# Linear attention with a mixture of experts: turned rows moved inside the chip's memory, loads issued by ScalarE into four places, small inputs read later

## The chip, the cores and the metric

The kernel runs on one core of a Trainium2 chip. The time is that of the device, in microseconds (us), median of several runs. A core has TensorE (PE in the rows, its weight loads PEld), VectorE (DVE), ScalarE (ACT), GpSimd (POOL) and SyncE (SP), each with its own in-order instruction stream, and 16 DMA engines that all of them share. PEq, ACTq, SPq and so on are the sequencers that issue transfers and wait.

## The reference, cut to what matters

Causal linear attention with a decay per head runs over 4 batches x 8 heads x 768 positions of 64 numbers; its output, 3072 tokens of 512 numbers, goes through a mixture of 8 experts, of which each token takes the best one.

```python
# attention, block by block (the kernel uses blocks of 128)
intra = einsum('bhic,bhjc->bhij', qb, kb) * Dmask;  intra = einsum('bhij,bhjd->bhid', intra, vb)
inter = einsum('bhid,bhde->bhie', qb * lam_pow, kv_state)
out[:, :, sl] = intra + inter
kv_state = lam_block * kv_state + einsum('bhsd,bhse->bhde', kb_dec, vb)
# x = out as [3072, 512]
logits = x @ w_gate + modality_bias[modality_id]
e_idx = argmax(logits);  gate_w = softmax(logits)[e_idx]
for e in range(8):
    h = maximum(x[mask_e] @ w1[e], 0)          # 512 -> 1024
    out[mask_e] = gate_w * (h @ w2[e])         # 1024 -> 512
```

## The kernel before, in words

**Attention.** There are 24 chunks of 128 tokens, done as 12 pairs (the loop over `m`, L812 to L889). `load(m)` (L86) brings the keys, queries and values of one pair, 2 MB, into one of six places (`SLOTS`, tag `load`); SP issues all of them, the one for pair `m + 6` in iteration `m`. In iteration `m` TensorE makes the `scores` (L243) of pair `m + 1`, then `from_state` (L277) and `values` (L285) of pair `m`, then `products` (L255, the new state) of pair `m + 1`. ScalarE scales keys (`kd`, L233) and takes results out of PSUM (`xt`, L288). VectorE applies the mask (L247), adds states (L265) and turns each result in 32x32 blocks (`turn`, L294, into one of four `xn` buffers).

**From attention to tokens.** `store` (L297) writes a turned chunk to the DRAM tensor `xs`, 256 KB, issued by ScalarE; `bring` (L306) reads it back as four transfers of 64 KB per token tile `row` (128 tokens x 528 numbers, eight buffers), issued by SP. The 24 token tiles form three groups of eight. For each group the gate is worked out on TensorE (`gates`), VectorE chooses the expert and the place of each token (`choose`, `ranks`, `slots_of`), and `one_slot` (L394) on POOL scatters a tile's rows to the DRAM tensor `placed`, sorted by expert. Eight `bring`s are issued in pair 5, eight in pair 10 and eight after tile 0.

**Experts.** Then come token tiles of 256 rows of one expert: four early ones (two from list A, made when group 0 is placed, two from list B, made after group 1), two thin ones (64 and 32 rows), eight wide ones, and more under a condition. `fetch_x(n)` reads the rows `xg` from `placed`, `fetch_w1` and `fetch_w2` the weights `raw1` and `raw2` (2 MB each, in four parts; where a tile's expert is that of the tile before, the transfer is skipped by a condition). `split` (L583) cuts each weight into a high part (ScalarE) and a low part (VectorE), `first_layer` (L674) and `second` (L698) multiply in three passes (`three`, L665), and POOL scatters the result to `out`. `raw1`, `raw2`, `w1h`, `w1l`, `w2h`, `w2l` lie in the six `load` places. `late_list` (L495) makes the list of all later tiles on VectorE, in pieces between the blocks of tile 2 (`amid2`, L930); its last result is `nums`, the count that every engine reads at L1015. `clear_ends` (L616) writes blank rows behind each expert's last token, eight transfers of 528 KB, each with a register loaded from `ends_at`.

**What sets the order.** PE, DVE, ACT and SP run in the order in which the code is written. On SP every instruction stands behind the one before it, waits included. The transfers of SP and ACT share eight completion counters, handed out in turn over both engines: a transfer waits until the one eight places earlier has landed.

```python
for m in range(pairs):
    ...
    if m == 0: gpsimd_constants(); routing_constants()   # L845, needs the small inputs mod and mb
    elif m == 5: ranks(...); four bring(c)               # L854
    if m + SLOTS < pairs: load(m + SLOTS)                # L858
    if m == 5: four more bring(c)
```

Of the kernel before, what the change touches and what calls it, by code (L numbers as in the profile page):

```python
# [15 lines left out]
P = 128  # L16
# [4 lines left out]
SLOTS = 6  # L21
# [13 lines left out]
ROWS = 8  # L35
# [8 lines left out]
def linear_attention_moe(tc, qkv, lam, modality, wg, mbias, w1, w2, out):  # L44
    nc = tc.nc
    with ExitStack() as ctx:
# [51 lines left out]
        busy = const.tile([P, DM], BF16, name="busy")  # L98
# [38 lines left out]
        for m in range(4, SLOTS):  # L137
            load(m)

# [8 lines left out]
        xs = dram.tile([N, DM], F32, name="xs")  # L148
# [148 lines left out]
        def store(g):  # L297
            xn = xns.pop(g).rearrange("q t p a -> q (t p a)")
            n = P // (1 + g % HB)
            for r in range(0, P, n):  # L300
                to = g * P + (r + P - n) % P
                nc.scalar.dma_start(out=xs[to : to + n, :], in_=xn[r : r + n])

        rows = {}

        def bring(c):  # L306

            grp, tb = divmod(c, 4)
            rows[c] = work.tile([P, RW], F32, name="row", bufs=ROWS)
            for t in range(4):  # L310
                g = 4 * grp + t
                nc.sync.dma_start(out=rows[c][t * Q : (t + 1) * Q, :DM].rearrange("a (j e) -> a j e", j=4),  # L312
                                  in_=xs[g * P : (g + 1) * P, tb * P : (tb + 1) * P].rearrange("(j a) e -> a j e", j=4))
# [80 lines left out]
        def one_slot():  # L394
            c, at = slots.pop(0)
            row = rows.pop(c)
# [237 lines left out]
        def fetch_regs(n, always=False):  # L634
            _, lst, i = tiles[n]
            er = nc.sync.value_load(item(lst, 0, i), min_val=0, max_val=E - 1)
# [5 lines left out]
        def fetch_w1(er, kw, to=None):  # L642
            for i in range(4):
                nc.sync.dma_start(out=(raw1 if to is None else to)[:, i],
                                  in_=w1[bass.ds(er, 1), :, i].rearrange("o p k f -> p (o k) f"), **kw)

        def fetch_w2(er, kw, to=None):
            for i in range(4):
                nc.sync.dma_start(out=(raw2 if to is None else to)[:, i],
                                  in_=w2[bass.ds(er, 1), :, 2 * i : 2 * i + 2].rearrange("o p f n -> p (o f) n"), **kw)  # L650
# [135 lines left out]
        w1_part = lambda nm, dt: slot([P, 4, KC, TT], dt, nm)  # L786
# [3 lines left out]
        aside = {8: (0, 2), 9: (1, 2), 10: (1, 2)}  # L790
# [21 lines left out]
        for m in range(pairs):  # L812
# [10 lines left out]
            elif m == 8:  # L823
                lgt = gate_rows()
            elif m == pairs - 1:
                routed = 1, *choose(1, lgt)
            if m == 0:
                keys(2)
                keys(3)
                store(0)  # L830
                store(1)
            if ahead:
                for i, g in enumerate((a + 2, b + 2)):
# [5 lines left out]
                    if i == 0 and m > 1:  # L839
                        store(a - 1)  # L840
            elif m > 0:
                store(a - 1)
            do()
            go(aside.get(m, (0, 0))[0])
            if m == 0:  # L845
                gpsimd_constants()
                routing_constants()
            else:
                from_state((a, b))
# [4 lines left out]
            elif m == 5:  # L854
                ranks(routed[-1])
                for c in range(RC // 2):
                    bring(c)
            if m + SLOTS < pairs:  # L858
                load(m + SLOTS)
            if m == 5:  # L860
                for c in range(RC // 2, RC):
                    bring(c)
            if m == pairs - 1:
                turn_rows(0)
                fetch_x(1)
            if m > 0:
                turn(a)
                store(a)
# [11 lines left out]
            elif m == 7:  # L880
                raw1 = w1_part("raw1", F32)
                fetch_w1(*fetch_regs(0, True))
            elif m == 8:
                raw2 = w2_part("raw2", F32)
                fetch_w2(*fetch_regs(0, True))
            elif m == 10:
                fetch_x(0)
                for c in range(RC, 2 * RC):
                    bring(c)  # L889
        store(B * NC - 1)  # L890
        w2h, w2l = w2_part("w2h", F32R), w2_part("w2l", F32R)
        w1h, w1l = w1_part("w1h", F32R), w1_part("w1l", F32R)
# [10 lines left out]
        def amid0(i):  # L903
            nonlocal routed, slots, early
            if i == 0:
                ranks(routed[-1])
                slots += slots_of(*routed)
                do()
                jobs.extend([("slots", one_slot)] * RC)
            elif i == 1:  # L910
                count()
                early = early_list("B", listB, early)
            elif i == 2:
                do()

        def amid1(i):
            nonlocal routed, slots, lgt
            if i == 0:
                lgt = gate_rows()
                routed = 2, *choose(2, lgt)  # L920
# [9 lines left out]
        def amid2(i):  # L930
            if i == 0:
                late_list(*early)
            elif i < 3:
# [12 lines left out]
        need("slots")  # L946
        fetch_x(2)
        fetch_w1(*fetch_regs(2))
        for c in range(2 * RC, 3 * RC):
            bring(c)  # L950
# [12 lines left out]
        first_layer(amid2)  # L963
        fetch_w2(*fetch_regs(3))
# [3 lines left out]
        clear_ends()  # L968
# [8 lines left out]
        both1 = w1_part("both1", F32)  # L977
# [17 lines left out]
        w1h = w1_part("w1h", F32R)  # L995
# [86 lines left out]
```

## Time and profile before

| | |
|---|---|
| median of 3 runs | 469.44 us (467.18 to 471.01) |
| the profiled execution | 467.61 us, of which its span is 465.8 us |
| busy: PE, DVE, ACT, POOL | 394.3, 264.9, 195.8, 99.2 us |
| mean granted TensorE clock | 0.923 of full speed |
| DMA | 87.96 MB in 56552 packets, mean 189 GB/s |

The span is the time from the first to the last instruction of the profiled execution; the rest of its time, 1.8 us, lies around it. Busy time of PE is modelled, and an engine that is not the bottleneck may idle at no cost. A row of a timeline gives start, length, engine, line, operation, the tile written <- the tiles read, and, in brackets, how long the engine had been idle and what it had waited for.

### The profile page before, as it was taken

How to read it: one execution, taken by the hardware profiler on the slowest of the kernel's cores; microseconds unless marked ns; L12 is line 12 of the kernel's file. 1: busy time of each engine (PE TensorE's matmuls, PEld its weight loads, DVE VectorE, ACT ScalarE, POOL GpSimd, SP SyncE). 2: the span in 40 equal slices, each digit the busy share in tenths (PEclk: the TensorE clock that was granted, in tenths of full speed). 3: DMA queues.
4: the chain of work that ended last, by engine and by line, in shares of the span. 5: the costliest groups of instructions: out<-in, count | busy, mean ns of one | idle time of the engine just before them, and what ended most of it. 6: DMA issues, size and time to landing. Idle time of an engine off the chain costs nothing.

```text
span 465.8 us, 9714 instructions
## 1 busy us (share of the span) xinstructions
PE 394.3 (85%) x3501; PEld 344.9 (74%) x3501; DVE 264.9 (57%) x494; ACT 195.8 (42%) x363; POOL 99.2 (21%) x125
## 2 busy tenths in 40 slices
PE   7849998894499689278984589999999999999991
PEld 4739987773388679276972169899999989898980
DVE  6446889742368653188712057666667575757520
ACT  1507483461043623134510054646555555646410
POOL 3722334360006605500210010202020202020200
PEclk8959999998599979769997799999999999999996
DMA  7999997889658886933532930777721121210100
GB/s 268 392 406 410 406 409 222 296 240 407 172 142 283 339 247 198 298 106 141 195 123 70 287 129 1 213 250 233 236 65 46 46 48 46 45 46 1 47 24 20
DMA packets 56552, 87.96 MB, mean 189 GB/s; under 512 B 9134, under 2 KB 34222, under 8 KB 56496
## 3 DMA queue, kind: packets, MB, share of 16 engines
q1 hardware_dynamic: 48928, 68.19, 44.4%
q0 software_dynamic: 3920, 12.78, 7.1%
q10 hardware_dynamic: 3648, 6.29, 3.8%
q8 instruction: 29, 0.48, 0.4%
q14 instruction: 27, 0.22, 0.1%
HBM read 96.86 MB, written 24.13 MB: 260 GB/s over the span
## 4 chain that ended last, share of the span: by engine, by line
issue 48%; DMA 26%; DVE 6%; POOL 6%; PE 5%; SPq 4%; ACT 2%; POOLq 0%; ACTq 0%; DVEq 0%
DMA raw<-in_w_dram 9%; DMA load<-in_qkv_dram 8%; POOL out_dram L710 5%; DMA row<-xs 5%; DMA xs<-xn 3%; SPq L312 3%; PE s L686 2%; DVE w2l L585 2%; PE kv L686 2%; DMA xg<-placed 1%; DVE hl L694 1%; ACT kd L233 1%; ACT w2h L584 1%; PE o L285 1%; PE s L243 1%
## 5 line engine op out<-in xcount | busy, mean ns | idle before, releaser
L585 DVE TENSOR_TENSOR w2l<-raw,w2h 128x1024 fp32r<-128x1024 f32 x48 | 58.8, 1224 | 51.0 <-ACT w2h L584 51.0
L666 PE MATMUL o<-w2h,hh 128*128 128x512 f32 x192 | 75.1, 391 | 0.0
L668 PE MATMUL o<-w2h,hl 128*128 128x512 f32 x192 | 74.9, 390 | 0.0
L667 PE MATMUL o<-w2l,hh 128*128 128x512 f32 x192 | 74.9, 390 | 0.0
L710 POOL DMA_INDIRECT out_dram<-y,idx x24 | 30.9, 1287 | 204.9 <-ACT y L709 175.4
L666 PE MATMUL kv<-xh,w1h 128*128 128x256 f32 x176 | 51.9, 295 | 11.4 <-DVE hl L694 11.4
L584 ACT CAST w2h<-raw 128x1024 fp32r<-128x1024 f32 x48 | 49.9, 1040 | 26.9 <-DMA raw<-in_w_dram 15.2
L585 DVE TENSOR_TENSOR w1l<-raw,w1h 128x1024 fp32r<-128x1024 f32 x44 | 51.1, 1220 | 5.2 <-ACT w1h L584 4.9
L667 PE MATMUL kv<-xl,w1h 128*128 128x256 f32 x176 | 51.5, 293 | 0.0
L666 PE MATMUL s<-xh,w1h 128*128 128x256 f32 x176 | 50.6, 288 | 1.0 <-ACT w1h L584 1.0
L668 PE MATMUL kv<-xh,w1l 128*128 128x256 f32 x176 | 51.2, 291 | 0.0
L668 PE MATMUL s<-xh,w1l 128*128 128x256 f32 x176 | 50.4, 286 | 0.8 <-DVE w1l L585 0.8
L667 PE MATMUL s<-xl,w1h 128*128 128x256 f32 x176 | 50.4, 286 | 0.0
L666 PEld LDWEIGHTS kv<-xh,w1h 128*128 128x128 f32 x176 | 35.0, 199 | 15.4 <-DVE hl L694 11.6
L584 ACT CAST w1h<-raw 128x1024 fp32r<-128x1024 f32 x44 | 43.0, 1046 | 3.3 <-DMA raw<-in_w_dram 3.3
L233 ACT ACTIVATE kd<-load,dk 128x64 f32<-128x64 f32 x144 | 35.9, 334 | 16.8 <-DMA row<-xs 6.5
L668 PEld LDWEIGHTS o<-w2h,hl 128*128 128x128 f32 x192 | 36.0, 188 | 7.6
L667 PEld LDWEIGHTS o<-w2l,hh 128*128 128x128 f32 x192 | 36.2, 188 | 7.2
L666 PEld LDWEIGHTS o<-w2h,hh 128*128 128x128 f32 x192 | 36.2, 188 | 7.2
L668 PEld LDWEIGHTS kv<-xh,w1l 128*128 128x128 f32 x176 | 35.3, 201 | 0.0
L666 PEld LDWEIGHTS s<-xh,w1h 128*128 128x128 f32 x176 | 33.8, 192 | 2.0 <-ACT w1h L584 1.4
L667 PEld LDWEIGHTS kv<-xl,w1h 128*128 128x128 f32 x176 | 35.1, 199 | 0.0
(217 smaller groups left out, 619.8 us busy)
## 6 DMA issues: line engine op xcount, KB each, us to landing
raw<-in_w_dram SPq DMA_DIRECT2D x104, 512.0 KB
load<-in_qkv_dram SPq DMA_DIRECT2D x9, 2048.0 KB
row<-xs SPq DMA_DIRECT2D x96, 64.0 KB
xg<-placed SPq DMA_DIRECT2D x48, 128.0 KB
placed<-blank SPq DMA_DIRECT2D x9, 528.0 KB
load<-in_qkv_dram SPq DMA_DIRECT2D x8, 512.0 KB
both<-in_w_dram SPq DMA_DIRECT2D x8, 512.0 KB
xs<-xn ACTq DMA_DIRECT2D x12, 256.0 KB
```

Of the source, the lines that this page charges most:

```text
L233: nc.scalar.activation(out=kds[g][:, p, hl, :], in_=kn[:, p, hl, :], func=AF.Copy, scale=dk[:, hl, p, P - 1 : P])
L243: nc.tensor.matmul(scs[g][:, hl, p, :], kt[r, p, :], qt[r, p, :], start=True, stop=True)
L285: nc.tensor.matmul(op[place(g, hl), p, :], vt[:, (2 * p + hl) * D : (2 * p + hl + 1) * D], pt[:, hl, p, :], start=(c == 0 and p == 0), sto ...
L312: nc.sync.dma_start(out=rows[c][t * Q : (t + 1) * Q, :DM].rearrange("a (j e) -> a j e", j=4), in_=xs[g * P : (g + 1) * P, tb * P : (tb + 1 ...
L584: nc.scalar.copy(out=hi, in_=src)
L585: nc.vector.tensor_tensor(out=lo, in0=src, in1=hi.bitcast(F32), op=ALU.subtract)
L666: nc.tensor.matmul(out, ah, bh, start=first, stop=False)
L667: nc.tensor.matmul(out, ah, bl, start=False, stop=False)
L668: return nc.tensor.matmul(out, al, bh, start=False, stop=last)
L686: mm = nc.tensor.matmul(hp[:, j, :], raw1[:, i, kc, fs], xt2[:, kc, :], start=(kc == 0), stop=(kc == KC - 1))
L694: nc.vector.scalar_tensor_tensor(out=hl[a][:, b], in0=hp, scalar=0.0, in1=hh[a][:, b].bitcast(F32), op0=ALU.max, op1=ALU.subtract)
L710: sc = nc.gpsimd.indirect_dma_start(out=out, out_offset=bass.IndirectOffsetOnAxis(ap=idx[:, t, 0:1], axis=0), in_=y, in_offset=None, bound ...
```

## The change

- `store` and `bring` go, and with them `xs`, `row` and their buffers. `spread(g)` copies a turned chunk straight from its `xn` buffer into the token tiles of its group, in the chip's memory: four transfers of 64 KB, each [32 partitions, 4, 128 numbers], issued by SP for every chunk as it is turned. A group's eight token tiles are one buffer (`grp`, three of them).
- `SLOTS` is 4 instead of 6. Pairs 0 to 3 are loaded by SP, pairs 4 to 11 by ScalarE, the one for pair `m + 4` in iteration `m`. `w1h`, `w1l` and `both1` take `grp` buffers. The first weights are fetched by ScalarE, one transfer of 2 MB each, in pairs 8 and 9 instead of by SP in pairs 7 and 8.
- `routing_constants` moves from pair 0 to pair 2; group 0 is scattered in pairs 7 to 9 instead of 8 to 10; group 1 is chosen in pair 8 and scattered in pair 11 (before: chosen in pair 11 and scattered during tiles 0 and 1). List B is made in pieces in tile 0.
- `clear_ends` stands ahead of `fetch_w2` of tile 3 instead of behind it, and `late_list` starts one block earlier in tile 2.

```diff
-SLOTS = 6
+SLOTS = 4
 def load(m):
     ...
-        nc.sync.dma_start(out=halves[m], in_=source(m))
+        (nc.sync if m < SLOTS else nc.scalar).dma_start(out=halves[m], in_=source(m))
-for m in range(4, SLOTS):
-    load(m)
-def store(g): ...
-def bring(c): ...
+def group(g):
+    n = B * NC // RN
+    if g % n == 0:
+        groups.append(work.tile([P, 2 * 4 * RW], F32, name="grp", tag="grp", bufs=RN))
+    return groups[g // n].rearrange("p (g c w) -> p g c w", g=2, c=4)[:, g % n // 4]
+def spread(g):
+    to = group(g)
+    xn = xns.pop(g).rearrange("q t p a -> q t (p a)")
+    t = g % 4
+    for j in range(4):
+        i = j ^ 2 * (g % HB)
+        nc.sync.dma_start(out=to[t * Q : (t + 1) * Q, :, i * P : (i + 1) * P], in_=xn[j * Q : (j + 1) * Q])
...
-aside = {8: (0, 2), 9: (1, 2), 10: (1, 2)}
+aside = {7: (1, 1), 8: (1, 2), 9: (1, 2), 11: (4, 4)}
...
     if m == 0:
         gpsimd_constants()
-        routing_constants()
     else:
+        if m == 2:
+            routing_constants()
...
-    elif m == 7: ... fetch_w1(*fetch_regs(0, True))
+    elif m == 8: ... fetch_w1(*fetch_regs(0, True, nc.scalar), eng=nc.scalar)
-    elif m == 8: ... fetch_w2(*fetch_regs(0, True))
+    elif m == 9: ... fetch_w2(*fetch_regs(0, True, nc.scalar), eng=nc.scalar)
...
 fetch_w1(*fetch_regs(2))
-for c in range(2 * RC, 3 * RC):
-    bring(c)
 first_layer(amid1)
 fetch_w2(*fetch_regs(2))
...
 first_layer(amid2)
+clear_ends()
 fetch_w2(*fetch_regs(3))
 turn_rows(3)
 split_rows()
 split_w1()
-clear_ends()
```

ScalarE in the middle of the attention loop, before (`xs<-xn` are the stores, `kd` the scaled keys, `xt` the results taken out of PSUM):

```order
L288 COPY xt<-o 128x512 x2
L302 DMA xs<-xn 128x512
L233 ACTIVATE kd<-load,dk 128x64 x8
L302 DMA xs<-xn 64x512 x2
L233 ACTIVATE kd<-load,dk 128x64 x8
```

and now, at the same place and up to the first weights (`raw_1378` is `raw1`):

```order
L283 COPY xt<-o 128x512 x2
L88 DMA load<-in_qkv_dram 128x4x1024
L228 ACTIVATE kd<-load,dk 128x64 x16
L334 ACTIVATE l<-l 128x64
L283 COPY xt<-o 128x512 x2
L631 TENSOR_LOAD listA
L631 ISA x2
L640 ISA
L640 DMA raw_1378<-in_w_dram 128x4096
```

Three stores a pair have left ScalarE's stream, and one load of 2 MB has come in behind the two copies.

SP from its first loads to the rows of tile 0, before:

```order
L89 DMA load<-in_qkv_dram 128x4x1024 x5
L613 DMA placed<-blank 256x1x528
L89 DMA load<-in_qkv_dram 128x4x1024 x2
L312 DMA row<-xs 32x4x128 x16
L89 DMA load<-in_qkv_dram 128x4x1024
L312 DMA row<-xs 32x4x128 x16
L636 TENSOR_LOAD listA
```

and now (`grp<-xn` are the spreads):

```order
L134 DMA mod<-in_modality_dram 128x48
L135 DMA mb<-in_mbias_dram 128x16
L308 DMA grp<-xn 32x4x128 x24
L608 DMA placed<-blank 256x1x528
L308 DMA grp<-xn 32x4x128 x60
L594 TENSOR_LOAD listA
```

The loads and the weights of tile 0 no longer stand between SP's small transfers.

SP in tile 2, before (`raw_1364` is `raw2`; the last part of `fetch_w2` of tile 3, then the clears):

```order
L649 DMA raw_1364<-in_w_dram 128x1024
L619 TENSOR_LOAD ends_at
L619 ISA x2
L613 ISA
L613 DMA placed<-blank 256x1x528
L619 TENSOR_LOAD ends_at
L619 ISA x2
L1015 TENSOR_LOAD nums
L1015 ISA x2
L613 ISA
L613 DMA placed<-blank 256x1x528
```

and now (`raw_1378` is `raw1`; the last part of `fetch_w1` of tile 3, then the clears):

```order
L643 DMA raw_1378<-in_w_dram 128x1024
L614 TENSOR_LOAD ends_at
L614 ISA x2
L608 ISA
L608 DMA placed<-blank 256x1x528
L614 TENSOR_LOAD ends_at
L614 ISA x2
L1008 TENSOR_LOAD nums
L1008 ISA x2
L608 ISA
L608 DMA placed<-blank 256x1x528
```

In both the read of `nums` stands behind the first of the eight clears; now the four parts of `fetch_w2` of tile 3 come after the eighth.

## Rows read from the trace of the kernel before

**Rows 1.** Stretches of 10 us: length, busy time by engine, granted clock, DMA share, GB/s

```profile
60.00:70.00 10.00, 9.93 (x188) 8.79 (x189) 8.18 (x15) 8.52 (x32) 3.72 (x3) 1.00 1.03 409
70.00:80.00 10.00, 8.80 (x188) 7.62 (x185) 9.45 (x31) 3.68 (x11) 5.09 (x7) 1.00 0.71 220
...
90.00:100.00 10.00, 7.38 (x99) 5.82 (x97) 3.28 (x8) 5.59 (x21) 4.85 (x6) 1.00 0.71 215
```

**Rows 2.** Timeline of SP in the attention stage and in tile 0

```profile
58.53 20.75 SPq L312 DMA_DIRECT2D row<-xs  x16
79.45 0.39 SPq L89 DMA_DIRECT2D load<-in_qkv_dram  x1
80.44 18.36 SPq L312 DMA_DIRECT2D row<-xs  x16
...
119.43 16.68 SPq L312 DMA_DIRECT2D row<-xs  x32
```

**Rows 3.** Timeline of TensorE in the attention stage

```profile
30.55 1.97 PE L277 MATMUL o<-qd,state 64*64 64x128 f32 x28 [6.75 <-DVE state L265]
...
99.67 2.06 PE L243 MATMUL s<-load 64*128 64x128 f32 x32
...
112.77 1.66 PE L319 MATMUL x<-xt,wgq 128*32 128x128 f32 x28 [3.82 <-ACT xt L288]
122.37 6.35 PE L686 MATMUL s<-xt,raw 128*128 128x256 f32 x16 [7.94 <-DVE xt L654]
```

**Rows 4.** Timeline of TensorE, tiles 2 and 3 and the first thin tile

```profile
180.35 0.28 PE L666 MATMUL s<-xh,w1h 128*128 128x256 f32 x1
...
200.51 0.58 PE L666 MATMUL kv<-xh,w1h 128*128 128x256 f32 x1 [11.36 <-DVE hl L694]
218.09 0.39 PE L666 MATMUL s<-xh,w1h 128*128 128x256 f32 x1 [0.99 <-ACT w1h L584]
...
251.29 5.38 PE L726 MATMUL s<-raw,xf 128*64 128x256 f32 x32 [8.03 <-DMA raw<-in_w_dram]
260.22 0.59 PE L726 MATMUL s<-both,xf 128*32 128x256 f32 x2 [3.54 <-DMA both<-in_w_dram]
```

**Rows 5.** DMA queues, of the page: packets, MB, share of 16 engines

```profile
q10 hardware_dynamic: 3648, 6.29, 3.8%
```

**Rows 6.** Stretches, columns as in rows 1: brings alone, then the first layer of tile 0

```profile
131.00:134.00 3.00, 3.00 (x16) 2.55 (x16) 2.27 (x6) 1.47 (x2) 1.15 (x1) 1.00 0.47 134
...
122.40:139.20 16.80, 16.80 (x75) 14.17 (x75) 9.67 (x29) 5.63 (x7) 1.15 (x1) 0.84 0.54 156
```

**Rows 7.** Chain that ended last: start, length, what; weights of tile 0

```profile
106.46 10.43 DMA raw<-in_w_dram
```

**Rows 8.** Timeline of SP, from tile 2 to the thin tiles

```profile
208.59 1.34 SPq L649 DMA_DIRECT2D raw<-in_w_dram  x4
210.75 24.34 SPq L613 DMA_DIRECT2D placed<-blank  x8
237.67 2.25 SPq L602 DMA_DIRECT2D xq<-placed  x4
```

**Rows 9.** Chain that ended last, in tile 2: late_list between the splits

```profile
200.46 0.07 DVE cntC L339
...
202.63 1.22 DVE w2l L585
...
204.46 0.09 DVE fewer L339
...
206.26 1.23 DVE w2l L585
207.48 0.60 DVE hl L694
...
214.38 0.17 DVE nums L339
```

**Rows 10.** Timeline of ScalarE at the end of tile 1

```profile
180.55 0.69 ACT L709 ACTIVATE y<-o,idx 128x512 f32<-128x512 f32 x1 [2.72 <-PE o L668]
```

More of the change, by code (lines that the diff above doesn't have):

```diff
@@ L96, in linear_attention_moe @@
             load(m)
-        busy = const.tile([P, DM], BF16, name="busy")
+        busy = work.tile([P, 2 * DM], BF16, name="busy", tag="qd", bufs=4)[:, :DM]
         nc.vector.memset(busy, 0.0)
@@ L295, in turn @@
                                 in_=xts[g].rearrange("q p (t a) -> q p t a", t=4))
[L297 to L313, printed above, removed]
+        groups = []
+        def group(g):
[10 more added lines that the diff above has]
+                nc.sync.dma_start(out=to[t * Q : (t + 1) * Q, :, i * P : (i + 1) * P], in_=xn[j * Q : (j + 1) * Q])
         def gates(grp):
@@ L395, in one_slot @@
             c, at = slots.pop(0)
-            row = rows.pop(c)
+            row = group(c // 4 * 4)[:, c % 4]
             pool(nc.gpsimd.tensor_copy(out=row[:, DM:].bitcast(I32), in_=pay[:, c, :]))
@@ L784, in keep_busy, with w1_part @@
                 nc.tensor.matmul(nothing, busy[:, :P], busy, start=(i == 0), stop=(i == n - 1))
-        w1_part = lambda nm, dt: slot([P, 4, KC, TT], dt, nm)
+        def w1_part(nm, dt, own=False):
+            if own:
+                part = work.tile([P, 2 * 4 * RW], dt, name=nm, tag="grp", bufs=RN)
+                return part[:, : 4 * KC * TT].rearrange("p (a k f) -> p a k f", a=4, k=KC)
+            return slot([P, 4, KC, TT], dt, nm)
         w2_part = lambda nm, dt: slot([P, 4, 2, DM], dt, nm)
         pairs = B * NC // HB
-        aside = {8: (0, 2), 9: (1, 2), 10: (1, 2)}
+        aside = {7: (1, 1), 8: (1, 2), 9: (1, 2), 11: (4, 4)}
         keep_busy(9)
@@ L829, in linear_attention_moe @@
                 keys(3)
-                store(0)
-                store(1)
+                spread(0)
+                spread(1)
             if ahead:
@@ L839, in linear_attention_moe @@
                     if i == 0 and m > 1:
-                        store(a - 1)
+                        spread(a - 1)
             elif m > 0:
-                store(a - 1)
+                spread(a - 1)
             do()
@@ L853, in linear_attention_moe @@
                 clear(slice(E * CAP, E * CAP + TT))
-            elif m == 5:
+            elif m == 5 or m == 9:
                 ranks(routed[-1])
-                for c in range(RC // 2):
-                    bring(c)
             if m + SLOTS < pairs:
                 load(m + SLOTS)
[L860 to L865, printed above, removed]
             if m > 0:
                 turn(a)
-                store(a)
+                spread(a)
             if ahead:
@@ L879, in linear_attention_moe @@
                 count()
-            elif m == 7:
+            elif m == 8:
                 raw1 = w1_part("raw1", F32)
-                fetch_w1(*fetch_regs(0, True))
-            elif m == 8:
+                fetch_w1(*fetch_regs(0, True, nc.scalar), eng=nc.scalar)
+            elif m == 9:
                 raw2 = w2_part("raw2", F32)
-                fetch_w2(*fetch_regs(0, True))
+                fetch_w2(*fetch_regs(0, True, nc.scalar), eng=nc.scalar)
             elif m == 10:
                 fetch_x(0)
-                for c in range(RC, 2 * RC):
-                    bring(c)
-        store(B * NC - 1)
+        turn_rows(0)
+        spread(B * NC - 1)
+        fetch_x(1)
         w2h, w2l = w2_part("w2h", F32R), w2_part("w2l", F32R)
-        w1h, w1l = w1_part("w1h", F32R), w1_part("w1l", F32R)
+        w1h, w1l = w1_part("w1h", F32R, True), w1_part("w1l", F32R, True)
         hh = [work.tile([P, 2, 2, TT], F32R, name=f"hh{i}", tag="pt", bufs=4) for i in range(2)]
```

55 lines of the change are left out of this document (27 added, 28 removed).

## The prediction

> **What bounds the kernel now.** I read the stretches first, then SP's timeline, then TensorE's waits, then the chain. Two points in time carry the sum: T0, the start of tile 0 on TensorE at 122.4 us, and T2, the start of tile 2 at 180.35 [rows 3, 4]. The wide tiles at the end keep TensorE full, and the change doesn't touch them.
>
> Up to T0 the DMA engines are the bound, with holes. From 60 to 70 us their share is 1.03 at 409 GB/s: full. From 70 to 80 and from 90 to 100 it is 0.71 [rows 1]. In these holes SP is going through brings, 16 in 20.75 us and 16 in 18.36, and the last load of 2 MB leaves only at 79.45, between them [rows 2]. Against a share of 1.00 the holes are 2 x 10 x 0.29 = 5.8 us. TensorE had stood still for 6.75 us before 30.55, for a VectorE that waited for the small inputs, and for 7.94 us before T0, for the rows of tile 0 [rows 3]. Those rows were asked for behind the weights, which landed at 106.46 + 10.43 = 116.9 [rows 7].
>
> From T2 to the first thin tile SP is the bound. Tile 2 stops for 11.36 us in its second block, since `fetch_w2` of tile 2 stands on SP behind 32 brings. Then the clears take SP 24.34 us, to 235.1, and only at 237.67 come the thin rows; the thin tile waits 8.03 us for its turn and then for `both1` [rows 4, 8].
>
> **The change part by part.**
>
> *DMA work up to T0.* The stores go: 6.29 MB in 3.8% of 465.8 us is 17.7 us of all engines, 0.74 per chunk [rows 5]. The eight brings of group 0 go: brings alone ran at 134 GB/s with a share of 0.47, so 285 GB/s at a full one, 0.92 us per chunk, 7.4 in all [rows 6]. 24 spreads come in. No row shows a transfer from on-chip memory to on-chip memory. The nearest is the bring, of the same 64 KB in the same 512-byte pieces to the same 32 partitions; below it stands the rate of the loads, 0.64 per chunk [rows 1], above it the pace at which SP got 16 brings out while loads were in flight, 18.36 / 4 = 4.6 per chunk [rows 2]. I take 0.92: 22.1 us. Net: 22.1 - 17.7 - 7.4 = -3.0.
>
> The 512-byte bring ran at 285 GB/s where the large loads ran at 409 [rows 1, 6]. The Trainium skill (DMA: Bandwidth & Descriptors, Specifications) gives 512 bytes as the size from which line rate is reached; this trace does not agree. By the page's rule the spreads would cost 24 x 0.64 = 15.4 us and the sum would be 6.7 lower.
>
> *The holes.* With the loads on ScalarE's queue none waits behind SP's small transfers. I book the 5.8 us as regained. What could take them: a load now waits for its place (four instead of six) and for the transfer eight places earlier, and behind it on ScalarE stand the scaled keys, for which TensorE's `products` wait. Between nothing and all, I take all, since the place of pair m is needed again only in pair m + 3.
>
> The Trainium skill (DMA: Bandwidth & Descriptors, Issuing engines are not separate DMA queues) says that issuing from several engines saves only the sequencer's issue time. Here a load took SP 0.39 us to issue, but stood behind 20.75 us of brings [rows 2], which the page doesn't count. By the rule the move of eight loads is worth 8 x 0.39 = 3.1 us instead of 5.8.
>
> *The rows of tile 0.* The weights leave SP for ScalarE, so the rows are not asked for behind them. The gates end at 112.77 + 1.66 = 114.4 [rows 3]; of the wait behind them the part up to 116.9 goes, 2.5 us, and the transfer itself stays. Tile 0 thus starts 3.0 + 5.8 + 2.5 = 11.3 earlier, at T0 = 111.1.
>
> *Small inputs later.* VectorE no longer waits for them in pair 0, and the 6.75 us of TensorE go. I count nothing for it: DMA is full there, and the loads are late next. Its price shows in the pace. Before, nine pairs took from 30.55 to 99.67, 7.7 us each, and T0 came 22.7 after that, 20.2 without the 2.5. Now the nine start at 23.8, and 111.1 - 20.2 - 23.8 = 66.9 leaves 7.4 per pair. If DMA were not the bound, the gates would end at 114.4 - 6.75 - 3.82 = 103.9, and T0 can't come sooner [rows 3].
>
> *Tile 0.* Its first layer ran at a mean clock of 0.84 over 16.8 us [rows 6]: after the wait TensorE worked at 1.2 instead of 2.4 GHz for a while, which cost 16.8 x 0.16 = 2.7 us. The wait shrinks from 7.9 to 5.4; I take half, 1.3. The scatters of group 1 now stand on POOL before T0; nothing on POOL is due before the result of tile 0, and the rows of tile 1 have the 14 us of tile 0's first layer. Tile 1 I leave as it is.
>
> *Tile 2 and the clears.* With no brings on SP, `raw2` is there at T2. The late list starts one block earlier, and its end, `nums`, sets SP free: it reads `nums` behind the first clear. VectorE: the result of tile 1 leaves ScalarE 0.9 after T2 [rows 10], and a cast of at most 1.2 follows: 2.1. Then four times a split and a low part, 1.23 + 0.60 each, 7.3. Then the list, 2.17 + 1.80 + 6.47 = 10.4 between the splits [rows 9]. `nums` is ready at T2 + 19.8. From `nums` (214.55) to the end of the clears (235.1) it took 20.5: T2 + 40.3. Now `fetch_w2` of tile 3, skipped, stands behind: 1.34 for its four parts [rows 8] and register reads, at most the 2.6 between the last clear and the thin rows; the thin rows go out at T2 + 44.2. Before it was 237.67 - 180.35 = 57.3. Gain 13.1.
>
> This has a price: tile 3 cannot split `raw2` before about T2 + 42.9, so TensorE stands still there for some 14 us, in place of the 11.36 in tile 2. From a stall of this kind to the end of tile 2 it took 218.09 - 200.51 = 17.6 with three blocks to go [rows 4]. With one block to go, and some 3.7 us of casts ahead of it (estimated from rows 9), tile 3 ends by T2 + 64 at the latest, and the first thin layer (5.38) by T2 + 69. `both1` used to come 260.22 - 237.67 = 22.6 after the thin rows, now T2 + 66.8. So SP's row is the later one, or TensorE by up to 2 us; I book nothing.
>
> *The rest at nothing:* `busy` in a shared buffer, w1 parts in `grp` buffers (their scatters are over 20 us before), one transfer for 2 MB of weights, and group 2's brings, which lie inside the stall already counted.
>
> **Sum.** 11.3 + 1.3 + 13.1 = 25.7. Against the profiled execution, 467.6 (span 465.8 and 1.8 around it), that makes 441.9; the median of the runs is 1.8 higher, so I forecast 443.
>
> **Rivals.**
>
> *The spreads run at the rate of the large loads.* For: nothing has to come from DRAM. Against: the brings' 285 GB/s. 443 - 6.7 = 436. This is the page's rule on 512 bytes as this kernel would show it.
>
> *The loads gain issue time only.* For: the DMA engines are shared, and four places bind the loads as the brings did. Against: the load at 79.45. 443 + 2.7 = 446. It is what the page's rule on issuing engines gives.
>
> *The clears are not held by `nums`.* They would start about T2 + 5, end by T2 + 29 and let tile 3 go: some 11 us earlier, 432. Against: the order, where the read of `nums` stands behind the first clear.
>
> *The spreads get the pace of the brings among loads*, 4.6 per chunk, 9.2 per pair [rows 2]. T0 = 23.8 + 9 x 9.2 + 20.2 = 126.8, 4.4 later than before, 15.7 than forecast: 459. For: SP still issues 96 of them, each waiting for the one eight places earlier, often a load. Against: they are spread over all pairs now.
>
> *Slower: loads and spreads of a pair run one after the other*, through the eight shared counters: the spread waits for the load, the next load on ScalarE for the spread, and the keys behind it. A load is 2.1 MB at 409 GB/s, 5.1 us; two chunks of spreads take 4.2 (32 brings in 16.68 without loads) to 9.2 [rows 1, 2]; a pair then 9.3 to 14.3, middle 11.8. T0 = 23.8 + 106.2 + 20.2 = 150.2, 39.1 later than forecast: 482. It decides from 10.8 per pair, where T0 is at 141.5 and the other gains of 14.4 and 1% are eaten.
>
> **How the numbers follow.** About 1% is what a measurement of this kernel can tell from no change. Chances: forecast 0.45, issue time only 0.13, spreads at load rate 0.12, clears free 0.05, pace of the brings 0.15, one after the other 0.10. All but the last two are faster by over 1% (below 465), and two thirds of the pace case: 0.85. The rest of that case, 0.05, is within 1%; 0.10 is slower. The range takes in the load-rate case, most of the free clears and most of the pace case: 427 to 462. Bounds of the spread's price lie inside it.
>
> **What would show it.** Right: tile 0 starts at 105 to 117; shares near 1 from 20 to 100 us; no TensorE wait near the second pair's state; no stall in the second block of tile 2; one of about 14 us in tile 3, ended by `raw2`; thin rows on SP some 44 us after T2. Wrong: spreads that take well over 1 us of all engines per chunk, ScalarE's keys waiting for landings in every pair, or tile 3 running through.

## The result, and the profile after

The changed kernel takes 473.73 us (median of 4 runs, 473.02 to 474.57), the kernel before, beside it, 468.97 (4 runs, 467.18 to 471.01): ratio 1.0101, 95% interval 1.0055 to 1.0147. It is about 1% slower; 443 was forecast, with 427 to 462 as the range.

TensorE after (timeline; columns as in [rows 3, 4]):

```profile
24.39 2.08 PE L238 MATMUL s<-load 64*128 64x128 f32 x16 [3.96 <-DMA load<-in_qkv_dram]
...
127.92 1.06 PE L314 MATMUL x<-xt,wgq 128*32 128x128 f32 x26 [0.34 <-ACT xt L283]
...
140.63 6.59 PE L688 MATMUL s<-xt,raw 128*128 128x256 f32 x16 [11.65 <-DVE xt L656]
...
197.94 0.28 PE L668 MATMUL s<-xh,w1h 128*128 128x256 f32 x1
...
245.26 0.58 PE L668 MATMUL kv<-xh,w1h 128*128 128x256 f32 x1 [13.57 <-DVE hl L696]
```

Tile 0 starts at 140.63 (T0), 18.3 later than before [rows 3]: the gates end at 129.0 instead of 114.4, and the wait behind them has grown from 7.9 to 11.65. From there on the kernel is quicker: T0 to the end of the span takes 330.7 instead of 343.4. Tile 2 starts at 197.94 (T2), with no stall in its second block [rows 4]; tile 3 stalls for 13.57.

SP after (timeline; `grp<-xn` are spreads, the eight `placed<-blank` the clears, `xq` the thin rows, [rows 2, 8]):

```profile
57.43 75.86 SPq L308 DMA_DIRECT2D grp<-xn  x60
134.66 1.93 SPq L597 DMA_DIRECT2D xg<-placed  x4
...
137.28 7.85 SPq L308 DMA_DIRECT2D grp<-xn  x12
...
177.07 6.28 SPq L651 DMA_DIRECT2D raw<-in_w_dram  x4
...
210.96 27.63 SPq L608 DMA_DIRECT2D placed<-blank  x8
240.43 1.21 SPq L651 DMA_DIRECT2D raw<-in_w_dram  x4
242.49 1.94 SPq L597 DMA_DIRECT2D xq<-placed  x4
```

The thin rows go out 242.49 - 197.94 = 44.55 after T2, against 57.3 before. The rows of tile 0 (`xg`) leave at 134.66, behind a row of 60 spreads that ends at 133.3.

The 10-us stretches after, to set beside [rows 1]:

```profile
60.00:70.00 10.00, 5.68 (x94) 4.87 (x91) 4.81 (x11) 3.14 (x11) 2.49 (x2) 0.90 0.85 232
70.00:80.00 10.00, 10.00 (x139) 8.72 (x137) 5.85 (x13) 3.84 (x15) 1.46 (x2) 0.76 0.80 253
...
90.00:100.00 10.00, 7.16 (x134) 5.92 (x133) 6.00 (x24) 1.20 (x4) 4.73 (x8) 1.00 1.00 334
```

The holes have not gone but spread: 232 GB/s at a share of 0.85 from 60 to 70 us, where it was 409 at 1.03. The whole stretch from 20 us to T0, first before, then after:

```profile
20.00:122.37 102.37, 77.31 (x1432) 67.48 (x1428) 62.55 (x156) 43.16 (x149) 31.18 (x34) 0.91 0.94 340
20.00:140.63 120.63, 93.53 (x1436) 80.75 (x1433) 63.79 (x160) 43.19 (x150) 31.64 (x36) 0.88 0.88 269
```

Share times length is the work of all DMA engines: 96.2 us before, 106.2 after. The rest, 6.1 and 14.5, they stood idle. So of the 18.3 us some 10 are more DMA work and some 8 more idle time.

Who waits, from 20 to 130 us (engine, line, releaser: total us, times, longest):

```profile
SPq L308 <- DMA load<-in_qkv_dram: 23.9, 7, 7.2
SPq L308 <- DMA grp<-xn: 23.7, 9, 4.8
...
ACT kd L228 <- DMA grp<-xn: 47.9, 8, 8.8
```

SP's spreads wait for loads, and ScalarE's scaled keys, behind a load in ScalarE's stream, wait for spreads, in every pair. So the loads come 10.9 us apart:

```profile
34.24 0.41 ACTq L88 DMA_DIRECT2D load<-in_qkv_dram  x1
...
99.60 0.38 ACTq L88 DMA_DIRECT2D load<-in_qkv_dram  x1
```

(the second load on ScalarE and the eighth, 65.4 us for six steps.) This is the picture of the slower rival. The question of the experiments: is it the waits of the transfers for one another, the price of the spreads on the DMA engines (the time for which these are busy with them), the places, or the queue they stand in?

### The profile page after: what moved, and what is told of

Its sections match the earlier page's. It is cut to its first block, busy times and chain, and to the rows that moved or that the text cites. A ratio compares the mean times of both kernels' runs of the same rounds, so it can differ in the third digit from the quotient of the medians.

```text
span 471.3 us, 9647 instructions
## 1 busy us (share of the span) xinstructions
PE 405.5 (86%) x3501; PEld 354.6 (75%) x3501; DVE 264.2 (56%) x494; ACT 194.7 (41%) x363; POOL 99.5 (21%) x125
## 4 chain that ended last, share of the span: by engine, by line
issue 47%; DMA 19%; PE 11%; DVE 8%; POOL 6%; SPq 4%; ACT 2%; POOLq 0%; ACTq 0%; DVEq 0%
DMA grp<-xn 8%; POOL out_dram L712 5%; DMA mod<-in_modality_dram 5%; DMA load<-in_qkv_dram 4%; SPq L308 2%; DMA placed<-blank 2%; PE s L688 2%; ACT kd L228 2%; PE o L668 2%; PE o L669 2%; PE o L670 2%; PE kv L688 1%; DVE pt L242 1%; DVE w2l L580 1%; DVE hl L696 1%
## 5 line engine op out<-in xcount | busy, mean ns | idle before, releaser
L580 DVE TENSOR_TENSOR w1l<-raw,w1h 128x1024 fp32r<-128x1024 f32 x44 | 51.3, 1222 | 4.5 <-ACT w1h L579 4.3
L668 PEld LDWEIGHTS kv<-xh,w1h 128*128 128x128 f32 x176 | 34.9, 198 | 17.6 <-DVE hl L696 13.8
L289 DVE STREAM_TRANSPOSE xn<-xt 128x512 f32<-128x512 f32 x24 | 17.0, 709 | 44.3 <-ACT xt L283 24.7
L250 PE MATMUL kv<-load,kd 128*64 128x64 f32 x320 | 31.1, 259 | 7.9 <-ACT kd L228 7.9
L215 POOL TENSOR_TENSOR qd<-load,pq 128x512 f32<-128x512 f32 x20 | 25.2, 1271 | 58.9 <-DMA load<-in_qkv_dram 41.9
```

The source lines that it names most:

```text
L215: pool(nc.gpsimd.tensor_tensor(out=qds[g], in0=loaded(g)[1], in1=pq, op=ALU.mult))
L250: nc.tensor.matmul(kp[r, g % HB, p, :], kd[:, p, hl, :], vt[:, (2 * p + hl) * D : (2 * p + hl + 1) * D], start=True, stop=True)
L289: nc.vector.transpose(out=xns[g].rearrange("q t p a -> q p t a"), in_=xts[g].rearrange("q p (t a) -> q p t a", t=4))
L580: nc.vector.tensor_tensor(out=lo, in0=src, in1=hi.bitcast(F32), op=ALU.subtract)
L668: nc.tensor.matmul(out, ah, bh, start=first, stop=False)
```

## The experiments

Unless said otherwise an experiment is an edit of the changed kernel and one run, and every timeline is one profile; "gates" is the end of the last gate matmul, T0 the start of tile 0: 129.0 and 140.6 there. Runs 1, 5 to 7, 9, 10, 13 and 18 don't give the experts the right rows; they serve the timing alone. Theory and rivals stand in the expectations, which were written before each group of runs.

**1. A quarter of the bytes.**

```diff
...
-out=to[t * Q : (t + 1) * Q, :, i * P : (i + 1) * P], in_=xn[j * Q : (j + 1) * Q]
+out=to[t * Q : (t + 1) * Q, :1, i * P : (i + 1) * P], in_=xn[j * Q : (j + 1) * Q, :1]
```

> Each of the 96 spreads carries a quarter of its bytes (one of the four rows of 512 bytes per partition; the rest of the row tiles is filled with zeros by VectorE, three fills); their number, order, queue and waits stay. The rows that the experts get are thus wrong in three quarters; the routing is not. Theory A (the eight shared completion counters pass loads and spreads on one after the other): the chain of waits stays as long as its landings, so tile 0 starts at 130 to 140 us, against 140.6. Theory B (the spreads' traffic itself: some 1.2 us of all DMA engines per chunk, and loads slowed beside them from 5.1 to 6.2 us): 24 x 1.2 x 0.75 = 21.6 us and most of 8 x 1.1 go, tile 0 starts at 110 to 119, and loads run at 380 GB/s or more of a full share.

Gates 114.2, T0 123.5, 457.25 us. T0 lies between the two theories: the bytes matter, but 9.3 us of wait for tile 0's rows are left.

**2. Loads with counters of their own.** `nc.scalar` becomes `nc.gpsimd` for loads 4 to 11.

> Loads 4 to 11 are issued by GpSimd, whose transfers have completion counters of their own; spreads stay on SP, all else too. No load waits for a spread any more, no spread for a load, and ScalarE's keys stand behind neither. Theory A (shared counters): the waits of SP for loads (24 us) and of ScalarE's keys for spreads (48 us) go, the pace falls from 10.9 to the 8.6 per pair that the DMA engines need (6.2 for the load, 2.4 for two chunks), so tile 0 starts near 140.6 - 9 x 2.3 = 120. Theory B (traffic): the DMA engines were at a share of 0.9 anyway; tile 0 starts at 134 to 141.

Gates 129.7, T0 138.6, 471.88 us: no gain at the gates. By itself this speaks against A. But something else waits now (SP, then VectorE, whose turn needs an `xn` buffer that a spread still reads):

```profile
SPq L310 <- DMA grp<-xn: 27.0, 22, 4.0
...
DVE xn L291 <- DMA grp<-xn: 20.6, 6, 6.1
```

Eight spreads a pair still share eight counters among themselves. And there was little idle time to win: from 20 us to the gates the share of the DMA engines is 0.95, against 0.91 in the changed kernel.

**3. Loads on SP again.** `nc.sync` for all loads.

> Loads 4 to 11 are issued by SP again, at the same place of the program, with four places as before. ScalarE's keys no longer stand behind a load that waits. Theory C (the waits of the keys behind the loads are the loss): TensorE's 7.9 us of waits for keys go, tile 0 starts near 132. Theory A: the counters still tie loads to spreads, in one queue now: 138 to 148. Theory B: the same traffic, 137 to 143.

Gates 143.4, T0 148.2, 483.02 us: later, at the end of A's range. C gets no support, but this is no clean test of it: the loads now stand behind the spreads on SP, and TensorE waits 31.4 us for loads, the keys 28.7.

**4. The price of a spread alone.** 32 transfers `away[t] <- made[j]` on SP in the third wide tile.

> 32 transfers of the spreads' form (64 KB each, from 32 partitions to 32 partitions of another quarter, in pieces of 512 bytes) are added on SP in the third wide tile, where the DMA engines are nearly idle: their price alone. Booked in the forecast: 0.92 us of all engines per four transfers, 285 GB/s at a full share. Theory A: 270 to 300 GB/s at a full share (the rest is waits). Theory B: 190 to 230 GB/s at a full share. The time of the whole kernel within 2 us of the changed kernel's.

```profile
344.00:354.00 10.00, 10.00 (x50) 8.45 (x49) 6.67 (x8) 6.22 (x8) 1.81 (x1) 1.00 0.48 115
```

115 / 0.48 = 240 GB/s, 1.09 us of all engines per 262 KB, between the two theories; the pieces turned out to be 2 KB, and 8 of the 32 transfers stay in their own partitions, so it isn't quite the spread. The whole took 482.4, not within 2 us, since the next weights stood behind the probe. Its attention part is that of the changed kernel, and its gates ended at 129.6 and its T0 was 144.1: between single profiles a few us of T0 mean nothing.

**5. Pieces of 2 KB.** `out=to[t * Q : (t + 1) * Q, i, :DM]`, one row.

> The changed kernel with each spread writing its four pieces of 512 bytes of a partition as one piece of 2 KB, into one row (so rows of the experts are wrongly put together; bytes, number, queue, order and waits of the spreads stay). Theory P (the small pieces make the spreads dear, 128 of them in each transfer): the mix of loads and spreads runs near the 400 GB/s of the loads alone, and tile 0 starts at 116 to 128 us. Theory S (traffic between two places on the chip is dear whatever its pieces): tile 0 within 4 us of 140.6. The probe alone, whose pieces turned out to be 2 KB, moved 103 GB/s at a share of about 0.42, 245 at a full one, which speaks for S.

Gates 125.1, T0 135.5, 467.41 us: T0 lies in neither range. Small pieces may cost something, not most.

**6. The source in DRAM.** `in_=w2[g % E, j * Q : (j + 1) * Q, :4, :P]`.

> The changed kernel with each spread reading 64 KB of w2 in DRAM, in the same pieces of 512 bytes to the same partitions, instead of the turned rows (which are left out of the row tiles; a spread then no longer waits for VectorE's turn). Theory S (source on the chip is what costs): spreads at the price of a bring, 0.92 us per chunk, tile 0 at 120 to 130 us. Theory P or any small transfer into 32 partitions beside loads: the mix stays at 300 to 335 GB/s at a full share, tile 0 at 136 to 144.

Gates 145.5, T0 146.4, 475.66 us. Up to T0 SP's queue took 29.0% of 126.4 = 36.7 us, (36.7 - 10.0) / 23.2 = 1.15 per chunk with the 10.0 of run 7 taken off, where the same working gives 1.28 for the changed kernel (below). So T0 is not late because both ends lie on the chip.

**7. No spreads.** The `for j` loop of `spread` goes.

> The changed kernel without the spreads: the row tiles are filled with zeros by VectorE (three tiles, two fills each), so the experts get empty rows. What remains up to tile 0 are loads, four places and TensorE's own work (75 us of it between 30 and 120 us before the change). Theory B (the spreads' traffic and what it does to the loads): loads land early, TensorE is the bound, tile 0 starts at 104 to 114 us, against 123.5 with a quarter of the bytes. Rival F (four places instead of six and the loads on ScalarE cost much by themselves): tile 0 at 118 or later.

```profile
108.63 1.06 PE L315 MATMUL x<-xt,wgq 128*32 128x128 f32 x26 [0.34 <-ACT xt L283]
110.56 3.72 PE L689 MATMUL s<-xt,raw 128*128 128x256 f32 x16 [0.87 <-DVE xt L657]
```

T0 110.56, 441.77 us. All 30 us of T0 come with the spreads; without them the four places, the loads on ScalarE and the later small inputs leave T0 within 0.6 of the forecast. F falls.

**8. The change's tile part on the kernel before.** The late list one block earlier, the second weights of tile 2 by ScalarE.

> The kernel before with its attention part (stores, brings, six places, loads on SP) and two things of the change's tile part: the late list begins one block earlier, and the second weights of tile 2 don't stand behind the brings of group 2 (one transfer of 2 MB, issued by ScalarE). The clears stay where they were. My theory of tile 2 (11.4 us of stall go; the list's end sets the clears free at about 20 us into tile 2, so that the thin rows go out 44 us into it, against 57 before): 13 us less, 452 to 458 us, ratio 0.965 to 0.98. Rival G (the brings of group 2 and their scatters hold the clears or the rows of tile 3 instead): 463 us or more, ratio 0.985 or above.

468.93 us (10 runs), ratio 1.0009 (0.9973 to 1.0045): nothing won. The stall in tile 2 went, but the brings now took SP 28.7 us, and tile 3 waited 7.2 for its weights and the first thin tile 15.3. The rival holds.

**9. Edits 1 and 2 together.**

> Both earlier edits together: spreads with a quarter of their bytes (rows three quarters zeros) and loads 4 to 11 issued by GpSimd with completion counters of their own. Without spreads tile 0 started at 110.6, with a quarter of the bytes at 123.5 although the DMA engines then had a share of only 0.78, with full bytes and loads on GpSimd at 138.6. Theory D (two limits close together: the chain load, spread, load through the counters, and the DMA time of the mix; taking one away alone leaves the other): with both gone tile 0 starts at 110 to 117. Rival (the counters don't matter, small transfers cost by their number): 120 to 126.

Gates 112.7, T0 119.7 (3.8 earlier than in run 1), 452.82 us. T0 lies between the two expectations, at the edge of the rival's. Not settled.

**10. All 128 partitions.** `nc.sync.dma_start(out=to[:, t, j * P : (j + 1) * P], in_=xn[:, j])`.

> The changed kernel with each spread of 64 KB going from 128 partitions to the same 128 partitions, one piece of 512 bytes each, instead of four pieces from 32 partitions to 32 others (rows of the experts are wrongly put together; bytes, pieces, number, queue and order stay). Theory K (all pieces of a transfer meet in a quarter of the partitions): spreads near 0.7 us per chunk, loads beside them near 370 GB/s, tile 0 at 118 to 128. Theory N (what counts is the number of small pieces, 512 of them per chunk): tile 0 at 137 to 144, spreads at 1.2 to 1.3 us per chunk.

Gates 123.0, T0 133.3, 466.12 us. With the pieces over all partitions the gates end 6.0 earlier (one profile on each side); K explains a part.

**11. Brings of group 2 earlier, in the kernel before.** Six of its eight rows ahead of `fetch_x(2)`, and the late list as in 8.

> The kernel before with two edits, all on its own queues: the late list begins one block earlier, and of the 32 brings of group 2 the first 24 are issued before the rows and first weights of tile 2, when SP has nothing else to do but wait for the scatters of group 1; the last 8 stay. In the run with loads of tile 2 by ScalarE the brings took SP 28.7 us instead of 20.2 and nothing was won. Theory (SP's queue in tile 1 is the limit; the second weights of tile 2 leave at about 177 instead of 190, the 11.4 us of stall become 0 to 3, the thin rows go out 44 to 47 us into tile 2): 453 to 460 us, ratio 0.967 to 0.985. Rival (the brings, each behind a scatter, push the rows of tile 2 back and TensorE waits there instead): 464 to 472, ratio 0.99 to 1.01.

466.44 us (10 runs), ratio 0.9978 (0.9951 to 1.0004). The thin rows left 4.4 us earlier than before, but tile 2 still stalled, for 8.2: the rows of tile 2 now left SP at 169.2, its second weights at 185.8. Nearly the rival.

**12. Tile 0's rows by GpSimd.**

```diff
...
+            if m == pairs - 1:
+                turn_rows(0)
...
-                fetch_x(0)
-        turn_rows(0)
+                fetch_x(0, nc.gpsimd)
```

> The changed kernel with the rows of tile 0 fetched by GpSimd (its queue holds no spreads, and the scatters of group 0 end on it at 106 us) instead of by SP behind 80 spreads, and turned by VectorE before the last two chunks instead of behind them. Theory (the 11.65 us that TensorE waits for tile 0 are SP's queue of spreads: gates end at 129.0, the last spread ahead of the rows leaves at 133.3, the rows land at 139.3): the wait falls to 1 to 3 us, tile 0 starts at 130 to 132, and the whole is 5 to 10 us shorter than the changed kernel, ratio to before 0.987 to 1.0; the pace of the pairs stays. Rival (the rows of tile 1, behind the last spreads and the scatters of group 1, take the wait over): tile 0 earlier, but tile 2 within 3 us of 197.9, ratio to before 1.005 to 1.015.

464.62 us (10 runs), ratio to before 0.9914 (0.9875 to 0.9953): the best complete kernel of the series.

```profile
133.82 1.06 PE L314 MATMUL x<-xt,wgq 128*32 128x128 f32 x26 [0.19 <-ACT xt L283]
134.81 3.72 PE L688 MATMUL s<-xt,raw 128*128 128x256 f32 x16
```

Tile 0 follows the gates without a wait. (They ended 5.9 later in this profile than in that of the changed kernel.) T2 is 189.6, 8.4 earlier. So the wait at T0 came from SP's row of spreads.

**13. Six places.**

> The changed kernel with six places for the loads, as before, and all spreads with their full bytes, form and order. The memory for it comes from the row tiles: all spreads write into one tile of four rows, and the scatters take an empty row, so the experts get empty rows; the parts of w1 lie in the places again, as before. The wait for tile 0's rows stays on SP behind the spreads. Theory P (the DMA time of the spreads as such: in five runs the gates end later by 0.58 us for each us of DMA time added to the run without spreads): gates end at 125 to 131, against 129.0 with four places. Theory F (four places hold no load in reserve, so that each delay of a load reaches TensorE; with six the loads run ahead as before): gates end at 112 to 119.

Gates 144.8, 505.16 us: unclear. The scatters, which share one row here, held GpSimd up and through its `qd` TensorE (12.8 us in one place), and VectorE waited 29.2 for spreads into the one shared tile. It gives no support to F, and no clean number.

**14. Clears behind the second weights of tile 3**, on top of 12.

> The run with tile 0's rows fetched by GpSimd, and the clears put back behind the second weights of tile 3. Forecast's step (tile 3's stall of 13 us behind the clears lies beside SP's own row of clears and thin rows and costs nothing, or up to 2 us): the stall goes, a wait of 8 to 14 us for the first thin tile's weights comes in its place, time within 3 us of that run's 464.6, ratio to before 0.985 to 0.996. Rival (the stall was the path): 455 to 459, ratio 0.97 to 0.98.

468.24 us (12 runs), ratio 0.9973 (0.9939 to 1.0006). The stall in tile 3 went, 9.2 of wait for the thin weights came in its place, the thin rows left 44.6 after T2 as ever: the tiles behave as forecast. It is 3.6 us slower than run 12: in its profile the gates, where the program doesn't differ, ended 5 later, after two waits of ScalarE before its last copies out of PSUM, 7.55 and 4.00 us, which the profile puts down to "remote"; in run 12 they are 4.50 and 1.13, for TensorE. Each comparison with before stands; the difference of the two I don't read. From T0 to the end of the span the two take 329.0 (14) and 330.3 (12).

**15. Spreads for group 0 only**, on top of 12; groups 1 and 2 by stores and brings.

> The run with tile 0's rows on GpSimd, with spreads for the 8 chunks of group 0 alone. Groups 1 and 2 go to DRAM by stores (SP, 0.74 us per chunk) and come back by brings into row tiles of their own: group 1 behind the attention part, group 2 behind the second weights of tile 1. Theory P (the DMA time of the spreads, 1.36 us per chunk with what they cost the loads, delays the gates by 0.58 of it; stores of before by 0.19): gates end at 109.7 + 0.58 x 10.8 + 0.19 x 11.8 = 118, tile 0 starts at 118 to 122, the whole takes 450 to 458 us, ratio 0.96 to 0.977. Rival (places and queues hold the pairs back, whatever carries the rows): gates at 126 or later, 460 us or more.

466.61 us (10 runs), ratio 0.9951 (0.9915 to 0.9988). Gates 119.2, T0 120.5, as worked out. In one kernel the two kinds of stretch stand side by side, first pairs with spreads, then pairs with stores:

```profile
30.00:70.00 40.00, 32.17 (x564) 28.70 (x561) 22.53 (x50) 15.17 (x53) 9.25 (x8) 0.93 0.82 233
90.00:110.00 20.00, 16.17 (x339) 14.51 (x337) 18.11 (x54) 9.95 (x38) 10.52 (x14) 1.00 1.02 401
```

The second stretch carries weights, since the last load left at 87.59. The loads alone leave 11.4 us apart beside spreads (34.38 to 68.60, three steps); the next three steps, beside stores, are 2.1, 10.0 and 7.0.

The whole won less than hoped: the brings came back on SP: stalls of 4.5 and 6.7 us in tiles 1 and 2, thin rows 51.3 after T2.

**16. Stores only**, the brings of group 0 among pairs 3 to 6.

> The same without any spread: all chunks by stores on SP, the brings of group 0 two rows per pair in pairs 3 to 6. Theory P: gates end at 110 + 0.19 x 25 = 114.5 as before the change, tile 0 at 115 to 119, 447 to 456 us, ratio 0.953 to 0.972. Rival (places and queues): gates at 124 or later, 458 us or more.

478.34 us (4 runs), ratio 1.0197 (1.0132 to 1.0261), gates 136.3. A clear miss: theory P, a price in DMA time, doesn't carry. Up to T0 the DMA engines do about the work of before (0.84 x 116.2 = 97.6 us, against 96.2), yet the gates end 22 us later. Eight brings stood in each of four pairs, between a load and the next, and these loads left 12.6 us apart (41.37 to 91.84, four steps). But one wait in the 22 us has another cause:

```profile
129.16 1.97 PE L272 MATMUL o<-qd,state 64*64 64x128 f32 x28 [10.18 <-POOL qd L215]
```

GpSimd made this `qd` late, behind the fetch of tile 0's rows, for which it had waited 12.32 us until scatters landed. So up to 10 us belong to the place of that fetch. Brings and spreads have in common that they are many; this run alone doesn't show that it is their number.

**17. 48 brings by GpSimd**, on top of 15.

> The run with spreads for group 0 alone, with 16 of the 32 brings of group 1 and all 32 of group 2 issued by GpSimd, with counters of its own; SP keeps 16. Theory (SP's queue in the tiles was what took the gain back): the weights of tiles 1 and 2 leave SP when their places are free, the stalls of 4.5 and 6.7 us go, tile 2 starts near 120.5 + 57 = 178, the thin rows leave 45 us later at 223, 452 to 459 us, ratio 0.963 to 0.98. Rival (the transfers themselves, 29 us of DMA time on top of the weights and rows, or GpSimd's own order, hold the tiles up): stalls in tile 1 or 2 stay, 463 us or more.

467.06 us (8 runs), ratio 0.9949 (0.9914 to 0.9984). The thin rows left at 230.05, 5.9 earlier than in 15 but 7 later than hoped, tile 1 stalled 6.4 for its weights' low part. Then some 5 us more were lost at the very end, as told in the last section.

**18. One transfer for a chunk instead of four**, on top of 10.

```diff
-for j in range(4):
-    nc.sync.dma_start(out=to[:, t, j * P : (j + 1) * P], in_=xn[:, j])
+nc.sync.dma_start(out=to[:, :, t * P : (t + 1) * P], in_=xn)
```

> The run whose spreads went between the same 128 partitions (e10_wide), with the four transfers of a chunk made one: 256 KB, 512 pieces of 512 bytes, the same bytes, pieces and partitions, but 3 transfers in a pair instead of 9, so that the transfer eight places earlier lies more than two pairs back (rows of the experts are wrongly put together). Theory chain (loads and spreads wait for one another): gates end at 110 to 115, against 123.0 with four transfers a chunk. Theory price (their DMA time, on top of the loads): 119 to 124. In between: both, in that proportion.

```profile
108.11 1.06 PE L312 MATMUL x<-xt,wgq 128*32 128x128 f32 x26 [0.34 <-ACT xt L283]
111.04 3.72 PE L686 MATMUL s<-xt,raw 128*128 128x256 f32 x16 [1.87 <-DVE xt L654]
```

Gates 109.2, T0 111.04, 442.98 us: the range of theory chain. The same bytes in the same pieces to the same partitions, and 13.8 us of the gates go, 22.2 of T0. From 20 us to T0, the stretch and SP's queue in it, first run 10:

```profile
20.00:133.26 113.26, 88.03 (x1439) 76.38 (x1436) 66.29 (x166) 43.39 (x150) 31.72 (x36) 0.91 0.85 287
...
q1 hardware_dynamic: 15230, 9.09, 26.4%
```

and run 18:

```profile
20.00:111.04 91.04, 75.79 (x1431) 66.67 (x1428) 62.63 (x159) 43.82 (x150) 31.79 (x36) 0.93 1.00 358
...
q1 hardware_dynamic: 14686, 9.36, 33.9%
```

SP's queue took about the same DMA time, 26.4% of 113.3 = 29.9 us and 33.9% of 91.0 = 30.9. What changed is the share of all engines, 0.85 to 1.00: the engines had stood idle for 17 us. The other 5 of the 22.2 are work: 96.3 us of all engines fell to 91.0, since ScalarE's queue, with the loads, took 53.6 us instead of 59.7. The waits are gone: in run 10 ScalarE's keys waited 41.5 us for spreads and SP 23.8 for loads; in run 18 the keys wait for no spread, and SP for loads:

```profile
SPq L306 <- DMA load<-in_qkv_dram: 2.4, 2, 1.3
```

And the loads come 6.9 us apart, where it was 10.9 in the changed kernel and 10.2 in run 10 (again the second on ScalarE and the eighth):

```profile
30.48 0.40 ACTq L88 DMA_DIRECT2D load<-in_qkv_dram  x1
...
72.12 0.38 ACTq L88 DMA_DIRECT2D load<-in_qkv_dram  x1
```

## Why the prediction was wrong

By its own sum, each part to the next mark (us):

| | forecast | measured |
|---|---|---|
| up to T0 | 111.1 | 140.6 |
| T0 to T2 | 56.7 | 57.3 |
| T2 to the thin rows | 44.2 | 44.6 |
| thin rows to the end of the span | 228.1 | 228.8 |
| around it | 1.8 | 1.7 |
| the profiled execution | 441.9 | 473.0 |

- **Tile 2 and the clears: right, step by step.** No stall in tile 2; `nums` ended at 218.2, T2 + 20.3 (19.8 forecast); the clears at 238.6, T2 + 40.7 (40.3); the stall moved to tile 3, 13.57 (some 14), and cost nothing that shows. Run 14 bears this out: without it a wait of 9.2 comes at the thin weights, and the tiles take 1.3 less in all.
- **Tile 0's clock: too small to matter.** The wait grew instead of shrinking, and the first block took 6.59 (granted clock 0.56 from 140.63 to 147.20) against 3.70 for the second; T0 to T2 came out 0.6 longer than forecast.
- **Small inputs later: right.** TensorE's wait for the state is gone; one of 3.96 for the load stands there, and the time isn't won.
- **The step that failed is "The holes": "Between nothing and all, I take all, since the place of pair m is needed again only in pair m + 3."** It looked at the places and not at the row of transfers. It forecast a pace of 7.4 us per pair; the loads came 10.9 apart, and instead of 5.8 us regained the DMA engines stood idle for 14.5 us up to T0, against 6.1 before. A pair now hands out nine transfers over eight counters. The waits show each load behind a spread, one spread of each pair behind a load, the keys behind the load on ScalarE, and VectorE's turns behind the spreads' buffers. Run 18 shows that their number matters: with three transfers a pair, at the same price of the spreads, the pace is 6.9 and T0 111.04. Of the 29.6 us between it and the changed kernel 13.8 come with the number of transfers (gates, run 10 to 18). That T0 and the whole, 442.98, meet the forecast's 111.1 and 443 so closely is luck: the forecast's gates, 111.1 - 5.4 = 105.7, are 3.5 too early, and its wait of 5.4 is 3.5 too long.
- **"The rows of tile 0": "the transfer itself stays" missed SP.** I took the weights out of the way of these rows and forgot that 80 spreads stood there now. Run 12 shows it: with the rows on GpSimd's queue the wait is gone. It was 11.65, against 1.87 in run 18, 9.8 of the 29.6; with 10.24 in run 10, the number of transfers on SP makes it too.
- **The price of a spread was mis-sized, 0.92.** SP's queue took 31.4% of 120.6 = 37.9 us up to T0, against 11.1% of 90.6 = 10.0 without spreads: 27.9 for 5.7 MB, 1.28 per chunk. With all 128 partitions it is (29.9 - 10.0) / 21.8 = 0.91, and with it go the last 6.0 of the 29.6. A net of -3.0 of DMA work was forecast; all engines did some 10 more. Besides the spreads' 5.8 (27.9 instead of 22.1) the loads cost more, which the sum had at nothing: ScalarE's queue took 50.5% of 120.6 = 60.9 us, against 62.2% of 90.6 = 56.3 in run 7.

The slower rival came nearest: it named the waits that the traces show, and 10.8 per pair as the point from which it decides; 10.9 was measured, and its sum then gives T0 = 23.8 + 9 x 10.9 + 20.2 = 142.1. Its own middle, 11.8 and 482 us, was too slow. It got a chance of 0.10: the argument against it counted places, and not a pair's nine transfers against the eight counters.

What is not shown: through which part the number acts. The waits point to the counters, but loads with counters of their own (run 2) gained nothing at full bytes; that the spreads' own row then takes over is read from its waits and was not tried apart. Nor were such counters tried with the spreads of run 10. SP's own time is another candidate: the 12 spreads behind the rows of tile 0 took it 7.85 us, 0.65 each, so a pair's eight 5.2.

The Trainium skill (DMA: Bandwidth & Descriptors, Rules for kernel authors) says to join many small transfers into one large. Run 18 agrees: 13.8 us of the gates go with a quarter of the transfers. The Trainium skill (DMA: Bandwidth & Descriptors, Why small descriptors are slow (HBM only)) exempts transfers within the chip's memory from the penalty on small pieces. Run 5 doesn't agree: with 2 KB pieces SP's queue took 27.4% of 115.5 = 31.6 us, (31.6 - 10.0) / 21.8 = 0.99 per chunk instead of 1.28.

## What to carry to other kernels

Count the transfers of one iteration, and what each waits for, before counting bytes. Here nine of them over eight counters waited for one another, and one transfer where there were four brought the forecast's time at the same price of the copies. (That form, as run 18 has it, doesn't put the rows where the experts need them; a kernel with it is not shown.) When an engine's queue gets a new row of small transfers, look for what urgent transfer stands behind it, and give that one to a queue that is empty. And a cost that is hidden where an engine is moved to may come back later: runs 8, 11 and 15 won a stall or an earlier tile and lost most of it behind brings on SP.

## What the runs showed of the hardware that was not expected

In these runs the end of the program is longer, the more transfers GpSimd issued. From the start of the last output scatter to the end of the span it takes 8.9 to 9.1 us in the kernels before and after and in run 7; 9.5 to 10.0 with 5 to 8 more transfers on GpSimd (runs 2, 9, 12, 14 to 16); and 14.7 in run 17, with 53 more:

```profile
core 0 of [0], span 465.6 us
...
450.91 0.98 POOL L729 DMA_INDIRECT out_dram<-y,idx  x1 [4.45 <-ACT y L728]
```

That is about 0.1 us for each, and in run 17 some 5 us. Why is not shown.
